# First chunk's scores by pairs of heads on the two halves of the rows, gates added by a selection product

## The chip, the cores and the metric

The kernel runs on one core of a Trainium2 chip. The metric is the device time of one execution in microseconds. PE is TensorE, DVE is VectorE, ACT is ScalarE, POOL is GpSimd, and SP is the engine whose queue issues most DMAs.

## The reference

Attention with forget gates over 2 batches of 8 heads, 576 tokens and 64 dimensions, then a mixture of 4 experts, then a gated layer. All inputs and outputs are float32.

```python
scores = (1 / sqrt(D)) * q @ k.T                       # B, H, S, S = 2, 8, 576, 576; D = 64
cum = cumsum(log(clip(f, 1e-4, 1)), axis=-1)
scores = where(causal, -1e9, scores + cum[..., :, None] - cum[..., None, :])
attn = exp(scores - max(scores)); attn = attn / (sum(attn) + 1e-9)
x = (attn @ v), heads side by side                     # 1152 tokens x 512
p = domain_probs / (sum(domain_probs) + 1e-9)
x = sum over 4 experts e of p[:, e] * (relu(x @ w1[e]) @ w2[e])
h = x @ w_in
out = (h * sigmoid(1.702 * h)) @ w_out
```

The query's own `cum` is the same for a whole row and drops out of the softmax, so the kernel adds only the key's.

## The kernel before

The work is cut into four chunks of tokens: the first 256 and the last 320 tokens of each batch (`CH`, line 20). Attention of a chunk is emitted in units, and the expert layers of a chunk follow when its eight heads are done. Large products are done in three products of rounded parts (`hi` and `lo`, in the type fp32r), the first chunk's scores in plain float32. A scheduling layer orders the instructions of each engine by its own estimate of their durations, so an edit in one place can move instructions in others. Instructions marked with `keep_in_program_order` stay in the order in which they are written.

The gates are prepared on 16 partitions, one per batch and head (lines 638 to 665): clip on DVE, logarithm on ACT, running sum on DVE (`cum`, in the tile `fr`), each in a first part of 256 and a second of 320 columns. After that the scaled sums go to DRAM (`cumd`), from where later chunks read them back to all partitions as `cb` and `cbs`.

The first chunk (`plain(c)`) works as follows. `load_plain` loads q and k of four heads each with 64 partitions as `qd` and `kd`, and v as `vd`. Partition 64 of `qd` holds a constant, and `load_plain_rest` writes the gate sums of four heads into partition 64 of `kd` by a DMA from ACT's queue, so that one product over 65 rows yields the score with its gate. A unit of the first chunk is one head with its two tiles of 128 queries (128 and 256 keys wide):

- `emit_scores` (line 394): the products on PE into one of two PSUM tiles `s`; `emit_max` (line 420): on DVE, mask and scale into `e`, with the row's maximum `mx`;
- `emit_exp` (line 434): on ACT, with the sum into `sm`; `emit_norm` (lines 440 to 443): reciprocal on DVE, and the product with it on POOL (this is called the normalization below);
- `emit_tr` (line 461): transposes on PE, taken to `ph` by ACT or DVE; `emit_pv` (line 491): the second products into `x`; `emit_x2` splits `x` into the halves `xh` and `xl`, and `emit_first` (line 581) multiplies them with the first expert's weights.

In the same stretch POOL rounds the next chunk's q and k (`khi`, `klo`, lines 50 and 333), adds a triangle to `cb` and `cbs` (lines 346 to 355) and sums the expert probabilities (`dps`, lines 259 to 264). Weights come in pairs of blocks as `wst` (line 142) and are split into `whi` (ACT or POOL) and `wlo` (DVE, line 163).

Of the kernel before, what the change touches and what calls it, by code (L numbers as in the profile page):

```python
# [7 lines left out]
F32 = mybir.dt.float32  # L8
# [3 lines left out]
ALU = mybir.AluOpType  # L12
PSUM = bass.MemoryType.PSUM

B, H, S, D = 2, 8, 576, 64
NT = B * S
DM = 512
SA = 256
# [4 lines left out]
WN = 384  # L23
WIDE = [NCH, NCH + 1, NCH + 2]
QW = 640
# [7 lines left out]
def attn_moe_mlp(ctx: ExitStack, tc: tile.TileContext, qk0, qk1, qk2, v0, vp, fg, dp, wa_moe, wb_moe, wa_mlp, wb_mlp, outT):  # L33
# [6 lines left out]
    nc = tc.nc  # L40
# [19 lines left out]
    h_p = pool("h", 2)  # L60
# [228 lines left out]
    def plain(c):  # L289


        return c == 0

    def load_plain(h0):
        G, wk = 4, SA
        qd, kd = ((h_p.tile([128, 4 * WN], F32, tag=t, name=n) if h0 else
                   kq_p.tile([128, S + QW], F32, tag="kq", name=n))[:, :G * wk].rearrange("p (g s) -> p g s", g=G)
                  for n, t in (("qd", "hh"), ("kd", "hl")))
        vd = v_p.tile([128, 2 * G * D], F32, tag="vd0", name="vd", bufs=2).rearrange("p (t g d) -> p t g d", t=2, g=G)
        for i, t in enumerate((kd, qd)):  # L300
            nc.sync.dma_start(out=t[0:64], in_=qk0[h0 // G, i].rearrange("d (g s) -> d g s", g=G))
        nc.sync.dma_start(out=vd, in_=v0[h0 // G].rearrange("p (t g d) -> p t g d", t=2, g=G))

        nc.gpsimd.memset(qd[64:65], 1.0 / NEG)
        groups[h0] = (qd, kd, vd)

    def load_plain_rest(h0):
        G, wk = 4, SA
        qd, kd, vd = groups[h0]
        nc.scalar.dma_start(out=kd[64:65], in_=cum[h0:h0 + G, :wk])  # L310
        for g in range(G):
            heads[0, h0 + g] = dict(vd=vd[:, :, g, :], qd=qd[:65, g], kd=kd[:65, g])

    def load_heads(p, h0):

# [40 lines left out]

    def units_of(c, h0):

        if plain(c):
            return [(c, ((h,), (0, 128))) for h in (h0, h0 + 1)]  # L360
        _, s0, n = CH[c]
        return [(c, ((h0, h0 + 1), (q0,))) for q0 in range(s0, s0 + n, 128)]

    sc, raw_s = {}, {}
    NEG = -1.0 / D ** 0.5

    def emit_scores(c, u):


        hs, tiles = u  # L370
        out = []
        for q0 in tiles:
            w = min(q0 + 128, S)
            if plain(c):
                st = heads[c, hs[0]]
                mm = [(0, w, [(st["qd"][:, q0:q0 + 128], st["kd"][:, :w])])]
            else:
                p = pass_of[c]
                hi, lo = (pairs[p, hs[0]][k] for k in ("hi", "lo"))
                if q0 < 512:  # L380
                    o = S + 128 + q0 - p[2]
                    zs = [(0, w, slice(64 * g, 64 * g + 64)) for g in range(2)]
                else:
                    o = S
                    zs = [(a, z, slice(0, 128)) for a, z in ((0, 288), (288, S))]
                mm = [(a, z, [(l[r, o:o + 128], k[r, a:z]) for l, k in ((hi, hi), (lo, hi), (hi, lo))]) for a, z, r in zs]
            pts = []
            for a, z, _ in mm:
                pts.append(ps_s.tile([128, 512], F32, tag="s", name="s"))
                out.append((q0, w, a, z, pts[-1]))  # L390
            n = len(mm[0][2])
            for i in range(n):
                for pt, (a, z, lr) in zip(pts, mm):
                    nc.tensor.matmul(pt[:, :z - a], lhsT=lr[i][0], rhs=lr[i][1], start=i == 0, stop=i == n - 1)  # L394
        raw_s[c, u] = out

    def emit_max(c, u):
# [77 lines left out]
    def emit_pv(c, h):  # L475

        if h % 2 == 0:
            return
        b, s0, n = CH[c]
        nk = (s0 + n + 127) // 128  # L480
        pt = xf[c, h // 2] = ps_t.tile([128, 512], F32, tag="t", name="x")
        for i in range(nk):
            o = max(0, 128 * i - s0)
            for g in range(2):
                ph = ph_of[c, h - 1 + g]
                if plain(c):
                    lhsT = heads[c, h - 1 + g]["vd"][:, i, :]
                else:
                    lhsT = pairs[pass_of[c], h - 1]["vd"][:, i, g, :]
                rhs = ph[:, i, o:n] if i < 4 else ph[:, 3, 0:64]  # L490
                nc.tensor.matmul(pt[64 * g:64 * g + 64, o:n], lhsT=lhsT, rhs=rhs, start=i == 0, stop=i == nk - 1)  # L491
# [152 lines left out]

    nc.scalar.activation(out=cum[:, :1], in_=ones[:, :1], func=AF.Ln)
    load_plain(0)
    load_plain(4)
    nc.gpsimd.memset(mask, 0.0)
    nc.gpsimd.affine_select(out=mask[:, 128:], in_=mask[:, 128:], pattern=[[-1, 128]],
                            compare_op=ALU.is_ge, fill=-1e10, base=0, channel_multiplier=1)  # L650
# [5 lines left out]
    for a, z in ((0, SA), (SA, S)):  # L656
        nc.vector.tensor_scalar(out=fr[:, a:z], in0=fr[:, a:z], scalar1=1e-4, scalar2=1.0, op0=ALU.max, op1=ALU.min)
        nc.scalar.activation(out=fr[:, a:z], in_=fr[:, a:z], func=AF.Ln)
        nc.vector.tensor_tensor_scan(out=cum[:, a:z], data0=ones[:, a:z], data1=fr[:, a:z],
                                     initial=cum[:, a - 1:a] if a else 0.0, op0=ALU.mult, op1=ALU.add)  # L660
        if a == 0:
            load_plain_rest(0)
            load_plain_rest(4)
    nc.vector.tensor_scalar(out=fr, in0=cum, scalar1=1.0 / NEG, scalar2=None, op0=ALU.mult)
    nc.scalar.dma_start(out=cumd, in_=fr)
    load_heads(passes[1], 0)
# [130 lines left out]
```

## Time and profile before

| | us |
|---|---|
| median of 3 runs | 737.4 |
| lowest of them | 736.33 |
| the profiled execution | 737.77 |
| its span, first to last instruction | 736.1 |
| PE busy | 715.6 (97%) |
| PE weight loads busy | 674.9 (92%) |
| DVE busy | 460.2 (63%) |
| POOL busy | 277.6 (38%) |
| ACT busy | 268.4 (36%) |
| HBM, mean over the span | 90 GB/s |

The busy times are sums over a span of unlike stages. What the first chunk is bound by can't be read from them; it takes the order of events in the first 40 us. A matmul's end is modelled, so the starts of PE's rows say more than their ends. A float32 product shows as two records, a product of the fp32r type as one. A row of the timeline merges instructions that follow one another; the name and shape in it are those of the first.

### The profile page before, as it was taken

Reading aid. Unit: us, or ns where it says so; the run is one execution under the profiler, and the core shown is the slowest. Engines: PE = TensorE matmul, PEld = TensorE weight load, DVE = VectorE, ACT = ScalarE, POOL = GpSimd, SP = SyncE. Lnnn points to the kernel's source line nnn. Section 1 sums busy time; section 2 is a strip of 40 time slices with the busy share of each in tenths; the row PEclk is TensorE's granted clock in tenths of the full one; section 3 lists DMA queues with packets and bytes.
Section 4 is the critical chain, followed back from the end, with each engine's and each line's share of the span. In section 5 each row is a group of like instructions: output and inputs, shape, how many; then the busy total and the mean of one; then the engine's idle time right before and its main releaser. Section 6 shows DMA issues by size and latency. Waiting matters only on the chain.

```text
span 736.1 us, 11924 instructions
## 1 busy us (share of the span) xinstructions
PE 715.6 (97%) x4488; PEld 674.9 (92%) x4488; DVE 460.2 (63%) x1023; ACT 268.4 (36%) x629; POOL 277.6 (38%) x345
## 2 busy tenths in 40 slices
PE   4999999999999999999999999999999999999998
PEld 3576788888899999999998999999999999999997
DVE  4785666575758999999999633445972124424422
ACT  4564554566542233222211221223354433323420
POOL 4886974653432022233232433232462222222220
PEclk9999999999999999999999999999999999999999
DMA  8776534332216464464443301000100000000012
GB/s 290 222 233 208 159 123 132 90 103 86 73 51 216 144 194 149 148 183 117 130 144 115 86 24 35 1 1 1 58 0 1 1 1 1 1 0 1 1 44 86
DMA packets 29496, 67.23 MB, mean 91 GB/s; under 512 B 3032, under 2 KB 4576, under 8 KB 29440
## 3 DMA queue, kind: packets, MB, share of 16 engines
q1 hardware_dynamic: 29392, 66.44, 28.9%
q8 instruction: 35, 0.57, 0.3%
q14 instruction: 21, 0.17, 0.1%
q10 hardware_dynamic: 48, 0.05, 0.0%
HBM read 64.05 MB, written 2.41 MB: 90 GB/s over the span
## 4 chain that ended last, share of the span: by engine, by line
PE 75%; DVE 13%; DMA 5%; issue 3%; POOL 3%; ACT 0%; ACTq 0%; DVEq 0%; POOLq 0%
PE m L604 32%; PE m L560 31%; PE s L394 5%; PE t L461 3%; PE x L491 3%; DVE wlo L163 3%; DMA mst<-in_wa_mlp_dram 2%; DMA mst<-in_wb_mlp_dram 2%; DVE cvd L226 1%; DVE wf L220 1%; DVE cvt L214 1%; DVE tmp L618 1%; DVE cvt L212 1%; DVE hl L587 1%; DVE wf L228 1%
## 5 line engine op out<-in xcount | busy, mean ns | idle before, releaser
L620 POOL TENSOR_TENSOR acc<-acc,tmp 128x384 f32<-128x384 f32 (+3 forms) x112 | 111.2, 1004 | 248.9 <-DVE tmp L618 238.0
L604 PE MATMUL m<-hh,wlo 128*128 128x384 f32 (+2 forms) x640 | 128.0, 320 | 1.4 <-DVE wlo L163 1.3
L604 PE MATMUL m<-hh,whi 128*128 128x384 f32 (+2 forms) x640 | 129.1, 321 | 0.0
L604 PE MATMUL m<-hl,whi 128*128 128x384 f32 (+2 forms) x640 | 127.7, 320 | 0.0
L560 PE MATMUL m<-xh,whi 128*128 128x384 f32 (+2 forms) x624 | 126.1, 322 | 0.4 <-DVE hl L587 0.2
L560 PE MATMUL m<-xl,whi 128*128 128x384 f32 (+2 forms) x624 | 126.2, 321 | 0.0
L560 PE MATMUL m<-xh,wlo 128*128 128x384 f32 (+2 forms) x624 | 126.2, 321 | 0.0
L53 ACT ACTIVATE whi<-wst 128x512 fp32r<-128x512 f32 x103 | 64.9, 631 | 119.8 <-PE m L560 58.0
L163 DVE TENSOR_TENSOR wlo<-wst,whi 128x512 fp32r<-128x512 f32 x112 | 93.3, 836 | 24.3 <-ACT whi L53 13.7
L604 PEld LDWEIGHTS m<-hh,wlo 128*128 128x128 f32 x640 | 105.6, 188 | 3.2 <-DVE wlo L163 2.4
L604 PEld LDWEIGHTS m<-hh,whi 128*128 128x128 f32 x640 | 105.8, 188 | 1.7 <-issue 0.7
L560 PEld LDWEIGHTS m<-xh,whi 128*128 128x128 f32 x624 | 103.1, 188 | 3.7 <-issue 1.7
L604 PEld LDWEIGHTS m<-hl,whi 128*128 128x128 f32 x640 | 105.9, 188 | 0.8 <-issue 0.5
L560 PEld LDWEIGHTS m<-xl,whi 128*128 128x128 f32 x624 | 103.8, 188 | 0.9 <-issue 0.7
L560 PEld LDWEIGHTS m<-xh,wlo 128*128 128x128 f32 x624 | 103.7, 188 | 1.1 <-issue 1.0
L595 POOL TENSOR_TENSOR hl<-tmp,hh 128x384 fp32r<-128x384 f32 x48 | 49.1, 1025 | 133.3 <-ACT hh L53 133.3
L586 ACT ACTIVATE hh<-m 128x384 fp32r<-128x384 f32 (+2 forms) x112 | 48.9, 436 | 117.5 <-PE m L560 117.5
L587 DVE SCALAR_TENSOR_TENSOR hl<-m,hh 128x384 fp32r<-128x384 f32 (+2 forms) x112 | 54.9, 493 | 34.9 <-ACT hh L586 34.9
L618 DVE TENSOR_TENSOR tmp<-m,dpb 128x384 f32<-128x384 f32 (+2 forms) x80 | 40.9, 512 | 38.4 <-PE m L604 32.0
L593 DVE TENSOR_TENSOR tmp<-m,sg 128x384 f32<-128x384 f32 x48 | 26.6, 554 | 54.2 <-ACT sg L592 54.2
L443 POOL TENSOR_SCALAR e<-e,sm 128x128 f32<-128x128 f32 (+4 forms) x72 | 47.4, 668 | 29.4 <-DVE sm L441 15.7
L434 ACT ACTIVATE e<-e,mx 128x128 f32<-128x128 f32 (+4 forms) x72 | 41.9, 583 | 35.9 <-DVE mx L420 34.9
(80 smaller groups left out, 742.6 us busy)
## 6 DMA issues: line engine op xcount, KB each, us to landing
wst<-in_wa_moe_dram SPq DMA_DIRECT2D x28, 512.0 KB, 3.5
wst<-in_wb_moe_dram SPq DMA_DIRECT2D x28, 512.0 KB, 3.8
mst<-in_wa_mlp_dram SPq DMA_DIRECT2D x16, 512.0 KB, 3.5
mst<-in_wb_mlp_dram SPq DMA_DIRECT2D x16, 512.0 KB, 3.6
cb<-cumd SPq DMA_DIRECT2D x16, 256.0 KB, 4.1
vd<-in_vp_dram SPq DMA_DIRECT2D x8, 320.0 KB, 13.1
kq<-in_qk_dram SPq DMA_DIRECT2D x4, 608.0 KB, 7.2
cbs<-cumd SPq DMA_DIRECT2D x8, 288.0 KB
```

Source lines behind the costliest of these rows:

```text
L53: nc.scalar.activation(out=out, in_=in_, func=AF.Copy)
L163: sub = nc.vector.tensor_sub(lf, raw, f(hf))
L394: nc.tensor.matmul(pt[:, :z - a], lhsT=lr[i][0], rhs=lr[i][1], start=i == 0, stop=i == n - 1)
L434: nc.scalar.activation(out=e[:, off:off + w], in_=e[:, off:off + w], func=AF.Exp, scale=-1.0, bias=mx, accum_out=sm[:, 0, k:k + 1])
L443: nc.gpsimd.tensor_scalar(out=e[:, off:off + w], in0=e[:, off:off + w], scalar1=sm[:, 0, i:i + 1], scalar2=1.0, op0=ALU.mult, op1=ALU.mult)
L560: nc.tensor.matmul(p[:, :n], lhsT=w[:, k, :], rhs=x[c][:, k, :], start=(j == 0 and k == 0), stop=(j == 2 and k == 3))
L586: nc.scalar.activation(out=hh[:, g, :n], in_=p[:, :n], func=AF.Relu)
L587: nc.vector.scalar_tensor_tensor(out=hl[:, g, :n], in0=p[:, :n], scalar=0.0, in1=f(hh[:, g, :n]), op0=ALU.max, op1=ALU.subtract)
L595: nc.gpsimd.tensor_sub(hl[:, g, :n], t[:, :n], f(hh[:, g, :n]))
L604: nc.tensor.matmul(p[:, :n], lhsT=w[:, k, :], rhs=x[:, k, :n], start=(j == 0 and k == 0), stop=(j == 2 and k == 3))
L618: nc.vector.tensor_mul(t[:, :n], p[:, :n], d)
L620: nc.gpsimd.tensor_add(a, a, t[:, z])
```

## The change

The gate row and the constant row go. q and k of a pair of heads now lie on the two halves of the partitions (head 0 on 0 to 63, head 1 on 64 to 127), and two pairs come with one DMA. The first chunk's gate sums are copied to partitions 0 to 15 (by ACT) and 64 to 79 (by DVE) of a zeroed tile `cum2`. A tile `sel` holds, for each pair, a row that picks the head's line of `cum2` on its half. A unit of the first chunk is now two heads with one tile of queries, as in the other chunks, and makes four float32 products over 64 rows: `sel` with `cum2` for the first head, for the second, then q with k for the first and for the second. The last three of them are kept in that order.

```diff
-    def load_plain(h0):
-        G, wk = 4, SA
...
-        for i, t in enumerate((kd, qd)):
-            nc.sync.dma_start(out=t[0:64], in_=qk0[h0 // G, i].rearrange("d (g s) -> d g s", g=G))
-        nc.sync.dma_start(out=vd, in_=v0[h0 // G].rearrange("p (t g d) -> p t g d", t=2, g=G))
-
-        nc.gpsimd.memset(qd[64:65], 1.0 / NEG)
-        groups[h0] = (qd, kd, vd)
-
-    def load_plain_rest(h0):
...
-        nc.scalar.dma_start(out=kd[64:65], in_=cum[h0:h0 + G, :wk])
...
+    def load_plain(k):
+
+        t = kq_p.tile([128, S + QW], F32, tag="kq", name="kq0")[:, :4 * SA].rearrange("p (g s) -> p g s", g=2)
+        vd = v_p.tile([128, 8 * D], F32, tag="vd0", name="vd", bufs=2).rearrange("p (t g d) -> p t g d", t=2, g=4)
+        nc.sync.dma_start(out=t, in_=qk0[2 * k:2 * k + 2].rearrange("g p s -> p g s"))
+        nc.sync.dma_start(out=vd, in_=v0[k].rearrange("p (t g d) -> p t g d", t=2, g=4))
...
-        if plain(c):
-            return [(c, ((h,), (0, 128))) for h in (h0, h0 + 1)]
...
-                st = heads[c, hs[0]]
-                mm = [(0, w, [(st["qd"][:, q0:q0 + 128], st["kd"][:, :w])])]
+
+                kq = groups[hs[0]][0]
+                mm = [(0, w, [(sel[r, h // 2, :], cum2[r, :w]), (kq[r, SA + q0:SA + q0 + 128], kq[r, :w])])
+                      for h, r in zip(hs, (slice(0, 64), slice(64, 128)))]
...
-                    nc.tensor.matmul(pt[:, :z - a], lhsT=lr[i][0], rhs=lr[i][1], start=i == 0, stop=i == n - 1)
+                    m = nc.tensor.matmul(pt[:, :z - a], lhsT=lr[i][0], rhs=lr[i][1], start=i == 0, stop=i == n - 1)
+                    if plain(c) and (i or pt is not pts[0]):
+                        tc.keep_in_program_order(m)
...
+    cum2 = h_p.tile([128, 4 * WN], F32, tag="hh", name="cum2")[:, :SA]
+    sel = h_p.tile([128, 4 * WN], F32, tag="hl", name="sel")[:, :4 * 128].rearrange("p (h q) -> p h q", h=4)
+    nc.gpsimd.memset(cum2, 0.0)
+    nc.gpsimd.memset(sel, 1.0 / NEG)
+    for g in range(2):
+        z = slice(64 * g, 64 * g + 64)
+
+        nc.gpsimd.affine_select(out=sel[z], in_=sel[z], pattern=[[-2, 4], [0, 128]], compare_op=ALU.is_equal,
+                                fill=0.0, base=-g, channel_multiplier=1)
...
-            load_plain_rest(0)
-            load_plain_rest(4)
+            nc.scalar.copy(out=cum2[:16], in_=cum[:, :SA])
+            nc.vector.tensor_copy(cum2[64:80], cum[:, :SA])
```

The order of the instructions changes with it. PE at the program's start, before; `s` are score tiles, `t` transposed ones, and a number tells buffers apart:

```order
L394 MATMUL s_175<-kd_131,qd_130 128x128 [waits DMAHW2_49,DMAHW5_49,DMAHW1_49,Pool_49]
L394 MATMUL s_177<-kd_131,qd_130 128x256
L394 MATMUL s_191<-kd_131,qd_130 128x128 [waits DVE_49]
L394 MATMUL s_193<-kd_131,qd_130 128x256 [waits DVE_49]
L394 MATMUL s_215<-kd_131,qd_130 128x128 [waits DVE_49]
L461 MATMUL t_202<-identr_124,e_179 128x128 [waits Pool_49]
```

PE at the same place now:

```order
L383 MATMUL s_175<-cum2_138,sel_139 128x128 [waits Activation_49,Pool_49]
L383 MATMUL s_176<-cum2_138,sel_139 128x128 [waits DVE_49,Pool_49]
L383 MATMUL s_175<-kq0_130 128x128 [waits DMAHW1_49]
L383 MATMUL s_176<-kq0_130 128x128
L383 MATMUL s_193<-cum2_138,sel_139 128x256 [waits DVE_49]
L383 MATMUL s_194<-cum2_138,sel_139 128x256 [waits DVE_49]
L383 MATMUL s_193<-kq0_130 128x256
L383 MATMUL s_194<-kq0_130 128x256
L452 MATMUL t_207<-identr_124,e_181 128x128 [waits Pool_49]
```

The first product waited for three DMAs and POOL; now it waits for ACT and POOL, the second for DVE and POOL, and only the third for a DMA.

POOL from its first normalization on, before (`khi` and `klo` are the next chunk's rounded keys and queries):

```order
L443 TENSOR_SCALAR e_179<-e_179,sm_180 128x128 [waits DVE_49,Activation_49]
L443 TENSOR_SCALAR e_179<-e_179,sm_180 128x256 [waits Activation_49]
L50 TENSOR_SCALAR khi_280<-kq_160 128x576 [waits DMAHW2_49]
L50 TENSOR_SCALAR khi_280<-kq_160 128x384
L333 TENSOR_TENSOR klo_281<-kq_160,khi_280 128x576 [waits Pool_49]
L443 TENSOR_SCALAR e_195<-e_195,sm_196 128x128 [waits DVE_49,Activation_49]
L443 TENSOR_SCALAR e_195<-e_195,sm_196 128x256 [waits Activation_49]
L333 TENSOR_TENSOR klo_281<-kq_160,khi_280 128x384 [waits Pool_49]
```

POOL from its first normalization on, now:

```order
L434 TENSOR_SCALAR e_181<-e_181,sm_182 128x128 [waits DVE_49,Activation_49]
L434 TENSOR_SCALAR e_181<-e_181,sm_182 128x128 [waits Activation_49]
L50 TENSOR_SCALAR khi_290<-kq_160 128x576 [waits DMAHW5_49]
L50 TENSOR_SCALAR khi_290<-kq_160 128x384
L322 TENSOR_TENSOR klo_291<-kq_160,khi_290 128x576 [waits Pool_49]
L322 TENSOR_TENSOR klo_291<-kq_160,khi_290 128x384 [waits Pool_49]
L434 TENSOR_SCALAR e_199<-e_199,sm_200 128x256 [waits DVE_49,Activation_49]
L434 TENSOR_SCALAR e_199<-e_199,sm_200 128x256 [waits Activation_49]
L259 TENSOR_TENSOR dps_339<-dpraw_169 128x9 [waits DMAHW2_49]
L261 TENSOR_TENSOR dps_339<-dps_339,dpraw_169 128x9 [waits Pool_49] x2
L434 TENSOR_SCALAR e_225<-e_225,sm_226 128x128 [waits DVE_49,Activation_49]
```

The second unit's normalization stood behind three of the four pieces of rounding and is now behind all four.

DVE around the first weight splits (`wlo`), before; line 420 is a maximum, with a second instruction that reads it out:

```order
L420 ISA e_274,mx_276<-s_270,ones_126 128x128 [waits Pool_49]
L420 ISA mx_276 128x1
L420 ISA e_274,mx_278<-s_272,ones_126 128x256
L420 ISA mx_278 128x1
L163 TENSOR_TENSOR wlo_650<-wst_171,whi_649 128x512 [waits DMAHW7_49,Activation_49]
L163 TENSOR_TENSOR wlo_653<-wst_171,whi_652 128x512 [waits Activation_49]
L440 TENSOR_SCALAR sm_275<-sm_275 128x2 [waits Activation_49]
L468 COPY ph_256<-t_260 128x2x128 [waits PE_49]
L441 RECIPROCAL sm_275<-sm_275 128x2 [waits DVE_49]
L263 RECIPROCAL dps_327<-dps_327 128x9 [waits Pool_49]
L420 ISA e_316,mx_318<-s_312,ones_126 128x128 [waits PE_49]
```

DVE around the first weight splits, now (`e_251` is the fourth unit's, `ph_205` and `ph_206` are the second unit's transposed tiles):

```order
L459 COPY ph_205<-t_231 128x2x128 [waits PE_49]
L263 RECIPROCAL dps_339<-dps_339 128x9 [waits Pool_49]
L163 TENSOR_TENSOR wlo_666<-wst_171,whi_665 128x512 [waits DMAHW3_49,Activation_49]
L163 TENSOR_TENSOR wlo_669<-wst_171,whi_668 128x512 [waits Activation_49]
L411 ISA e_251,mx_253<-s_245,ones_126 128x256 [waits PE_49]
L411 ISA mx_253 128x1
L163 TENSOR_TENSOR wlo_672<-wst_173,whi_671 128x512 [waits DMAHW4_49,Activation_49]
L163 TENSOR_TENSOR wlo_675<-wst_173,whi_674 128x512 [waits Pool_49]
L411 ISA e_251,mx_255<-s_246,ones_126 128x256 [waits PE_49]
L411 ISA mx_255 128x1
L459 COPY ph_206<-t_235 128x2x128 [waits PE_49]
```

The splits came behind the fifth head's maxima; now two stand ahead of each of the fourth unit's two maxima.

## Rows read from the trace of the kernel before

**Rows 1.** Busy time by stretch: bounds, length, busy us (instructions), granted clock, DMA, GB/s.

```profile
20.00:30.00 10.00, 9.39 (x45) 5.38 (x44) 7.84 (x32) 5.91 (x23) 9.60 (x21) 1.00 0.70 220
...
200.00:400.00 200.00, 199.71 (x1358) 196.08 (x1358) 182.93 (x356) 56.27 (x116) 52.52 (x52) 1.00 0.46 142
```

**Rows 2.** Timeline of PE from 9 us: start, length, instruction, count, idle before.

```profile
10.13 3.79 PE L394 MATMUL s<-kd,qd 65*128 65x128 f32 x10 [10.13 <-DMA cumd<-fr]
```

**Rows 3.** Timeline of ACT and its DMA queue (ACTq), 0 to 14 us.

```profile
4.72 1.81 ACTq L310 DMA_DIRECT2D kd<-fr  x2
...
7.05 1.28 ACT L434 ACT_TABLE_LOAD   x1 [2.58 <-DVE fr L664]
11.26 0.40 ACT L434 ACTIVATE e<-e,mx 128x128 f32<-128x128 f32 x1 [2.93 <-DVE mx L420]
...
12.25 0.51 ACT L434 ACTIVATE e<-e,mx 128x256 f32<-128x256 f32 x1 [0.49 <-DVE mx L420]
```

**Rows 4.** Timeline of DVE, 0 to 30 us.

```profile
3.89 1.78 DVE L659 TENSOR_TENSOR_SCAN fr<-ones,fr 16x256 f32<-16x256 f32 x2
5.71 0.45 DVE L664 TENSOR_SCALAR fr<-fr 16x576 f32<-16x576 f32 x1
10.93 0.29 DVE L420 CUSTOM_DVE_ANT_0 e<-s,ones 128x128 f32<-128x128 f32 x1 [4.78 <-PE s L394]
...
11.79 0.42 DVE L420 CUSTOM_DVE_ANT_0 e<-s,ones 128x256 f32<-128x256 f32 x1 [0.56 <-PE s L394]
...
15.70 0.42 DVE L468 COPY ph<-t 128x256 f32<-128x256 f32 x1
...
20.09 1.38 DVE L163 TENSOR_TENSOR wlo<-wst,whi 128x512 fp32r<-128x512 f32 x2
```

**Rows 5.** Timeline of POOL, 0 to 40 us.

```profile
2.42 0.29 POOL L649 TENSOR_SCALAR_AFFINE_SELECT ones<-ones 128x128 f32<-128x128 f32 x1
...
13.43 0.82 POOL L443 TENSOR_SCALAR e<-e,sm 128x128 f32<-128x128 f32 x2 [8.64 <-DVE sm L441]
14.22 1.15 POOL L50 TENSOR_SCALAR khi<-kq 128x576 fp32r<-128x576 f32 x2
15.33 1.41 POOL L333 TENSOR_TENSOR klo<-kq,khi 128x576 fp32r<-128x576 f32 x1
...
17.51 1.00 POOL L333 TENSOR_TENSOR klo<-kq,khi 128x384 fp32r<-128x384 f32 x1
...
20.25 1.28 POOL L261 TENSOR_TENSOR dps<-dps,dpraw 128x9 f32<-128x9 f32 x2
...
37.48 0.82 POOL L443 TENSOR_SCALAR e<-e,sm 128x128 f32<-128x128 f32 x2
```

**Rows 6.** DMA issues, whole span and 0 to 45 us: count, size, us to landing.

```profile
wst<-in_wa_moe_dram SPq DMA_DIRECT2D x28, 512.0 KB, 3.5
...
kd<-in_qk_dram SPq DMA_DIRECT2D x2, 256.0 KB, 3.6
```

**Rows 7.** PE's groups by shape, 10 to 21.9 us, then 21.9 to 30 us: busy, mean ns.

```profile
L394 PE MATMUL s<-kd,qd 65*128 65x256 f32 x10 | 5.7, 676 | 0.1
L394 PE MATMUL s<-kd,qd 65*128 65x128 f32 x10 | 3.3, 434 | 10.1 <-DMA cumd<-fr 10.1
...
L394 PE MATMUL s<-kd,qd 65*128 65x256 f32 x6 | 1.9, 397 | 0.0
L394 PE MATMUL s<-kd,qd 65*128 65x128 f32 x6 | 1.4, 308 | 0.0
```

**Rows 8.** Timeline of PE, next chunk's scores: 42 us, then 59 us.

```profile
42.16 0.44 PE L394 MATMUL s<-khi 64*128 64x384 f32 x1
...
59.18 0.44 PE L394 MATMUL s<-khi 64*128 64x384 f32 x2
59.46 0.34 PE L394 MATMUL s<-khi,klo 64*128 64x384 f32 x2
59.63 0.34 PE L394 MATMUL s<-klo,khi 64*128 64x384 f32 x2
```

More of the change, by code (lines that the diff above doesn't have):

```diff
@@ L292, in plain @@
         return c == 0
-    def load_plain(h0):
-        G, wk = 4, SA
[L296 to L299, printed above, removed]
-        for i, t in enumerate((kd, qd)):
-            nc.sync.dma_start(out=t[0:64], in_=qk0[h0 // G, i].rearrange("d (g s) -> d g s", g=G))
-        nc.sync.dma_start(out=vd, in_=v0[h0 // G].rearrange("p (t g d) -> p t g d", t=2, g=G))
-        nc.gpsimd.memset(qd[64:65], 1.0 / NEG)
-        groups[h0] = (qd, kd, vd)
-    def load_plain_rest(h0):
-        G, wk = 4, SA
-        qd, kd, vd = groups[h0]
-        nc.scalar.dma_start(out=kd[64:65], in_=cum[h0:h0 + G, :wk])
-        for g in range(G):
-            heads[0, h0 + g] = dict(vd=vd[:, :, g, :], qd=qd[:65, g], kd=kd[:65, g])
+    def load_plain(k):
[4 more added lines that the diff above has]
+        for g in range(2):
+            groups[4 * k + 2 * g] = (t[:, g], vd[:, :, 2 * g:2 * g + 2, :])
     def load_heads(p, h0):
@@ L486, in emit_pv @@
                 if plain(c):
-                    lhsT = heads[c, h - 1 + g]["vd"][:, i, :]
+                    lhsT = groups[h - 1][1][:, i, g, :]
                 else:
@@ L646, in attn_moe_mlp @@
     load_plain(0)
-    load_plain(4)
+    load_plain(1)
+    cum2 = h_p.tile([128, 4 * WN], F32, tag="hh", name="cum2")[:, :SA]
+    sel = h_p.tile([128, 4 * WN], F32, tag="hl", name="sel")[:, :4 * 128].rearrange("p (h q) -> p h q", h=4)
+    nc.gpsimd.memset(cum2, 0.0)
+    nc.gpsimd.memset(sel, 1.0 / NEG)
+    for g in range(2):
+        z = slice(64 * g, 64 * g + 64)
+        nc.gpsimd.affine_select(out=sel[z], in_=sel[z], pattern=[[-2, 4], [0, 128]], compare_op=ALU.is_equal,
+                                fill=0.0, base=-g, channel_multiplier=1)
     nc.gpsimd.memset(mask, 0.0)
@@ L759, in first @@
     def first(k, q):
-        a = np.stack([k[0, :, :SA], q[0, :, :SA]]).reshape(2, 2, 4, SA, D)
-        return a.transpose(1, 0, 4, 2, 3).reshape(2, 2, D, 4 * SA)
+        return np.concatenate([a[0, :, :SA].transpose(0, 2, 1).reshape(4, 2 * D, SA) for a in (k, q)], axis=-1)
     def pairs(k, q, s0):
```

## Prediction

> **What bounds the kernel now.** I read the table of stretches first. From 200 us to 400 us PE is busy for 199.71 of 200 us [rows 1]: there the end is the sum of PE's work, and any gain has to be made earlier. The order of the two programs agrees: their last 3,016 products on PE, nearly all of what comes behind 200 us, are the same in the same order. So the change can move the end only by moving the moment at which PE reaches that common stretch.
>
> I then read the start, engine by engine. PE's first product begins at 10.13 us, after a wait that fills the whole time before it [rows 2]. The row names the DMA of `cumd` as releaser, but the product waits for the loads of `kd` and `qd` and for the gate row written into `kd` by ACT's queue. DVE has the first half of the scan by about 4.7 us (the scan row starts at 3.89 us and holds both halves, 1.78 us together), ACT's queue issues the two gate DMAs between 4.72 us and 6.53 us, and the loads of q and k, issued from 1.26 us on, take 3.6 us [rows 3, 4, 6]. So the gate DMA comes last: 5.4 us pass between the scan's first half and the first product.
>
> After that, two views matter. POOL waits 8.64 us for its first normalization at 13.43 us and is then nearly never free: 9.60 of the 10 us from 20 to 30 us [rows 1, 5]. Its last normalization of the first chunk ends at 38.30 us (37.48 us + 0.82 us) [rows 5]. I take that moment as the mark by which a lead of the new kernel is measured, because PE's transposes, the second products and the first expert's products follow it. And PE is slow until about 21.9 us: a 256-column record of the scores lasts 676 ns before and 397 ns after, a 128-column one 434 ns and 308 ns [rows 7]. [...]
>
> **The change part by part.**
>
> *The gate DMAs go; a copy on ACT and one on DVE replace them.* An activation of 128 columns took 0.40 us, a copy of 256 columns on DVE 0.42 us [rows 3, 4]. The two run side by side behind the scan's first half, so `cum2` is ready at about 4.7 + 0.05 + 0.42 = 5.2 us. The other inputs: q and k of the first four heads now come in one DMA of 512 KB, issued at the same 1.26 us; the nearest rows are 3.5 us to landing for the weight loads of that size and 3.6 us for the load of `kd` [rows 6], so 4.8 to 4.9 us, at worst 6 us since it is twice as large as the latter. The selection tile needs two selections of 512 columns on POOL, whose first selection of 128 columns began at 2.42 us and took 0.29 us [rows 5]; a wider one costs between 0.29 and 4 x 0.29 = 1.16 us, so the tile is ready between 3.3 and 5.0 us and hides. I take 5.9 us for PE's first product: 4.2 us earlier.
>
> *What gives back the first part.* ACT's second table load stood behind the issue of `cumd` and began at 7.05 us for 1.28 us [rows 3]. The issue waits for DVE's scaled gates, which ended at 6.16 us and now come 0.42 us later because the copy stands ahead of the second half of the scan [rows 4]. The two gate issues that went before it cost 1.81 us of ACT's queue and are gone, but they were not last. So the table is still in place only at about 8.3 us, and the first exponential starts there instead of at 11.26 us. From the first exponential to POOL's first normalization it was 13.43 - 11.26 = 2.17 us, 0.49 us of which ACT waited for a second maximum [rows 3, 5]; in the new unit both maxima (0.29 us each) are there by then. First normalization: 8.3 + 2.17 - 0.49 = 10.0 us, a lead of 3.4 us.
>
> *The products.* A pair of heads had two products per tile, one behind the other, over 65 rows. It now has four, in the order selection of the first head, selection of the second, q of the first, q of the second, the two heads on different halves of the rows. Where the old kernel alternates such halves, its trace shows both at once: six 384-column products begin as three pairs at 59.18, 59.46 and 59.63 us, and the first pair of them lasts the same 0.44 us that a single one takes at 42.16 us [rows 8]. So I cost the 16 added products at nothing. If the halves did not overlap, they would be as dear as the 16 there are: 5.7 + 3.3 + 1.9 + 1.4 = 12.3 us of PE [rows 7].
>
> Going from 128-row to 64-row products is not free: the first of those steps lasts 59.46 - 59.18 = 0.28 us, the second 59.63 - 59.46 = 0.17 us [rows 8]. Transposes and second products use all 128 rows, so the eight units make some nine changes in and nine out: 18 x 0.11 = 2.0 us at the upper clock, which were not there before. I take none of it, since a unit's second pair waits for DVE's maxima anyway, and keep 2.0 us for the range. [...]
>
> *What the new order gives back later.* A lead of 3.4 us on POOL would reach the mark whole if nobody waited. The order shows a knot at the fourth unit (second tile of heads 2 and 3). POOL now does all four pieces of the next chunk's key rounding before the second unit's normalization: 1.15 + 1.41 + 1.00 = 3.56 us [rows 5]. With the first unit's normalization (0.8 us, the row for 128 and 256 columns is 0.82 us) that makes 10.0 + 0.8 + 3.56 = 14.4 us; then the second unit's (0.9 us by the same row, for 512 columns), the probability sums (1.28 us) and the third unit's (0.7 us, for 256): 17.3 us. The transposes that wait for the second unit stand on PE between the two selection products of the fourth unit. On DVE the probabilities' reciprocal, which needs POOL at 17.3 us, stands ahead of two weight splits (1.38 us), the fourth unit's first maximum (0.42 us), two more splits (1.38 us) and the second maximum (0.42 us) [rows 4, 5]: 17.3 + 3.6 us, and an estimated 0.3 us for the reciprocal and the steps between, make 21.2 us. In the old trace DVE has five heads' maxima and two splits behind it at 20.09 + 1.38 = 21.5 us [rows 4]; now it has four heads and four splits at 21.2 us. Two splits more (1.38 us) and one head less (0.29 + 0.42 us) make 0.7 us, and 0.3 us in time: a lead of about 1.0 us.
>
> So between 1.0 us (DVE's order sets the mark) and 3.4 us (POOL alone does). POOL's fourth normalization needs DVE's fourth pair of maxima, so the lower end is nearer: I take 1.5 us. DMA bytes stay as they were; the stretch behind the mark is shuffled by the scheduler, with the same work in it, at nothing.
>
> *The sum.* The profiled execution took 737.77 us (span 736.1 us); 737.77 - 1.5 = 736.3 us. The median of the runs is 0.4 us lower than that execution, inside what I can resolve.
>
> **The rivals.**
>
> *The lead passes whole* (chance 0.25): the knot dissolves because POOL waits less elsewhere. For it: POOL is the fullest engine from 20 to 30 us. Against it: DVE's splits stand ahead of POOL's next input. 737.77 - 3.4 = 734.4 us.
>
> [...]
>
> *The halves don't overlap* (0.05), the change not doing what it says: half of the 12.3 us is hidden at best, so 737.77 - 1.5 + 6 to 12 = 742 to 748 us. Rows 8 speak against it.
>
> **How the numbers follow.** My forecast, 736.3 us with a range of its own from 734.8 to 738.2 us, has 0.50; the whole lead 0.25, the slower knot 0.17, no overlap 0.05, the rest 0.03. The range from 731.0 us (whole lead and an earlier clock) to 740.5 us (the knot) leaves out the lack of overlap and the rest. Two per cent, about what a measurement of this kernel can tell from no change, is 14.8 us; no case but the last reaches it. Faster 0.02, same 0.95, slower 0.03.
>
> **What would show it.** Right: the first score product near 5.9 us, ACT's second table load still near 7 us, POOL's first normalization near 10 us, score products of the two heads starting together, and the first chunk's last normalization between 35 and 37.5 us. Wrong: a first product near 10 us (loads were last, not the gates), products one behind the other, a fourth unit's maximum well before 19 us or after 23 us, or the common stretch reached with a lead or lag other than at the mark.

## The result, and the profile after

The changed kernel takes 744.88 us (median; 742.53 to 746.58), the kernel before 737.22 us beside it: a ratio of 1.0091, 95% interval 1.0063 to 1.0118. (One of the old kernel's four executions took 1168.98 us; without it their median is 737.04 us.) The change is slower by 7.7 us: less than the 2% (14.8 us) that I took as the least a measurement can tell, but clear of the noise by its interval, and outside my range. The profiled execution is the slowest of the four, 746.58 us (span 744.9 us), so its waits may be somewhat longer than those of a median execution.

The table of stretches of the changed kernel, with the columns of [rows 1]:

```profile
0.00:13.00 13.00, 5.58 (x26) 3.91 (x26) 6.71 (x22) 6.47 (x16) 7.49 (x19) 1.00 0.84 307
...
20.00:30.00 10.00, 9.40 (x51) 6.03 (x51) 5.27 (x27) 4.60 (x19) 8.02 (x17) 1.00 0.45 134
30.00:40.00 10.00, 4.43 (x15) 2.72 (x16) 3.28 (x11) 1.09 (x4) 4.07 (x9) 0.69 0.69 198
40.00:60.00 20.00, 20.00 (x126) 15.21 (x127) 11.81 (x46) 11.38 (x31) 11.48 (x20) 0.90 0.46 162
...
200.00:400.00 200.00, 199.07 (x1356) 194.81 (x1356) 178.52 (x355) 58.15 (x122) 55.55 (x54) 1.00 0.46 142
```

The same stretch of 30 to 40 us in the kernel before:

```profile
30.00:40.00 10.00, 9.08 (x48) 5.79 (x47) 7.13 (x23) 3.75 (x11) 7.60 (x14) 1.00 0.73 220
```

One row stands out. From 30 to 40 us PE is busy for 4.43 us (9.08 us before), POOL for 4.07 us, and the granted clock is 0.69 of full: it reads 1.00 in every stretch up to 33 us and 0.50 in each microsecond from 34 to 44 us (0.95 in the one ahead, 0.93 in the one behind). Below, the lower level is this 0.50, or a stretch in which records last as long as there: a 256-column second product (`x<-ph,vd`) takes 653 ns (mean) from 33.9 to 44.1 us, 671 ns from 10 to 22 us, where the clock reads 1.00, and 404 ns from 46 to 60 us. From 20 to 30 us PE is as busy as it was (9.40 us against 9.39 us), and the common stretch behind 200 us is nearly as full (199.07 us against 199.71 us) [rows 1]. The timeline of PE shows the start and the stall:

```profile
4.93 0.90 PE L383 MATMUL s<-cum,sel 64*128 64x128 f32 x4 [4.93 <-ACT cum L663]
...
20.19 0.58 PE L383 MATMUL s<-cum,sel 64*128 64x128 f32 x1 [0.47 <-DVE mx L411]
20.19 0.58 PE L383 MATMUL s<-kq 64*128 64x128 f32 x1
...
23.21 1.23 PE L383 MATMUL s<-cum,sel 64*128 64x256 f32 x4
24.23 1.06 PE L383 MATMUL s<-kq 64*128 64x256 f32 x4
...
28.45 0.70 PE L383 MATMUL s<-cum,sel 64*128 64x256 f32 x4
28.99 0.60 PE L383 MATMUL s<-kq 64*128 64x256 f32 x4
35.23 1.14 PE L452 MATMUL t<-identr,e 128*128 128x128 f32 x4 [5.65 <-POOL e L434]
36.27 0.58 PE L572 MATMUL m<-xh,whi 128*128 128x256 f32 x1
...
57.39 0.73 PE L551 MATMUL m<-xh,whi 128*128 128x256 f32 x4
```

The first product starts at 4.93 us, 5.2 us before the old one [rows 2], released by the copy on ACT. Products of the two heads start together (20.19 us). Then PE stands 5.65 us at 29.6 us for a normalization by POOL. POOL's own timeline says why:

```profile
9.41 0.72 POOL L434 TENSOR_SCALAR e<-e,sm 128x128 f32<-128x128 f32 x2 [4.75 <-DVE sm L432]
...
21.37 0.94 POOL L434 TENSOR_SCALAR e<-e,sm 128x256 f32<-128x256 f32 x2 [1.21 <-DVE mx L411]
...
28.95 0.45 POOL L338 TENSOR_TENSOR cb<-cb,tri 128x128 f32<-128x128 f32 x1
33.90 0.70 POOL L344 TENSOR_TENSOR cbs<-cbs,tri 64x64 f32<-64x64 f32 x2 [4.50 <-DMA cbs<-cumd]
34.70 0.93 POOL L434 TENSOR_SCALAR e<-e,sm 128x256 f32<-128x256 f32 x2
...
36.19 1.15 POOL L434 TENSOR_SCALAR e<-e,sm 128x128 f32<-128x128 f32 x2
...
39.79 0.93 POOL L434 TENSOR_SCALAR e<-e,sm 128x256 f32<-128x256 f32 x2 [1.86 <-DVE sm L432]
```

The first normalization comes 4.0 us earlier than in [rows 5]. By the fourth unit's normalization this lead is gone: four heads are then normalized at 22.31 us (21.37 + 0.94 us). In the kernel before, the same four heads were done at 20.28 us:

```profile
19.46 0.82 POOL L443 TENSOR_SCALAR e<-e,sm 128x128 f32<-128x128 f32 x2
```

POOL had other work in between (the next `khi` at 18.15 us, which the old kernel has at 29.16 us). Then POOL stands 4.50 us at the triangle add on `cbs` for that tile's load, and the first chunk's last three normalizations come behind it in its row: DVE had the reciprocals of the first two by 27.35 and 29.22 us, and they begin at 34.70 and 36.19 us. The last ends at 40.72 us, where the old kernel's ended at 38.30 us [rows 5].

The kernel before has the same late load, in its POOL and PE timelines:

```profile
35.29 0.71 POOL L355 TENSOR_TENSOR cbs<-cbs,tri 64x64 f32<-64x64 f32 x2 [2.25 <-DMA cbs<-cumd]
```

```profile
30.58 0.38 PE L581 MATMUL m<-xh,whi 128*128 128x256 f32 x1
...
49.27 0.50 PE L560 MATMUL m<-xh,whi 128*128 128x256 f32 x2
```

There only the last head's normalizations stand behind the add, and PE has the first expert's products to do. So the lag is 36.27 - 30.58 = 5.7 us at the first expert's first product (L572, before L581) and 57.39 - 49.27 = 8.1 us at the first product of the common code (L551, before L560). At the end it is 8.8 us (spans of 744.9 us and 736.1 us).

### The profile page after: what moved, and what is told of

Read it like the earlier page. It is cut to its first block, busy times and chain, and to the rows that moved or that the text cites. A ratio compares the mean times of both kernels' runs of the same rounds, so it can differ in the third digit from the quotient of the medians.

```text
span 744.9 us, 11979 instructions
## 1 busy us (share of the span) xinstructions
PE 720.9 (97%) x4520; PEld 679.1 (91%) x4520; DVE 457.2 (61%) x1024; ACT 269.0 (36%) x630; POOL 277.3 (37%) x347
## 4 chain that ended last, share of the span: by engine, by line
PE 61%; DVE 15%; DMA 12%; POOL 6%; issue 5%; ACT 0%; ACTq 0%; SPq 0%; DVEq 0%; POOLq 0%
PE m L595 28%; PE m L551 26%; DMA mst<-in_wb_mlp_dram 5%; DMA mst<-in_wa_mlp_dram 4%; PE s L383 3%; DVE wlo L163 3%; DVE cvd L226 2%; PE x L482 2%; DVE cvt L212 2%; PE t L452 2%; POOL klo L322 2%; POOL e L434 2%; DVE cvt L214 1%; DVE cvt L223 1%; DMA cbs<-cumd 1%
## 5 line engine op out<-in xcount | busy, mean ns | idle before, releaser
L551 PE MATMUL m<-xh,whi 128*128 128x384 f32 (+2 forms) x624 | 127.2, 323 | 0.9 <-DVE hl L578 0.8
L551 PE MATMUL m<-xh,wlo 128*128 128x384 f32 (+2 forms) x624 | 126.0, 321 | 0.0
L551 PE MATMUL m<-xl,whi 128*128 128x384 f32 (+2 forms) x624 | 124.9, 320 | 0.0
L551 PEld LDWEIGHTS m<-xh,whi 128*128 128x128 f32 x624 | 103.1, 188 | 4.6 <-issue 2.3
L551 PEld LDWEIGHTS m<-xh,wlo 128*128 128x128 f32 x624 | 103.8, 188 | 0.6 <-issue 0.4
L551 PEld LDWEIGHTS m<-xl,whi 128*128 128x128 f32 x624 | 103.6, 188 | 0.4 <-issue 0.4
L434 POOL TENSOR_SCALAR e<-e,sm 128x128 f32<-128x128 f32 (+4 forms) x72 | 45.0, 636 | 33.2 <-DVE sm L432 25.9
```

What stands on the lines that cost most here:

```text
L434: nc.gpsimd.tensor_scalar(out=e[:, off:off + w], in0=e[:, off:off + w], scalar1=sm[:, 0, i:i + 1], scalar2=1.0, op0=ALU.mult, op1=ALU.mult)
L551: nc.tensor.matmul(p[:, :n], lhsT=w[:, k, :], rhs=x[c][:, k, :], start=(j == 0 and k == 0), stop=(j == 2 and k == 3))
```

## Experiments

Theory A: POOL's row, with a `cbs` add that waits for a slow load ahead of the normalizations, makes the loss. Rival B: the new products make it (changes between halves, records at the lower level at the start). Times are medians; each run is compared with the kernel before, timed on the same chip at 735.9 to 738.0 us.

**Each `cbs` load as two DMAs**

```diff
-nc.sync.dma_start(out=st["cbs"], in_=cumd[r:r + 2, :].unsqueeze(1).to_broadcast([2, 64, S]))
+for g in range(2):
+    nc.sync.dma_start(out=st["cbs"][64 * g:64 * g + 64], in_=cumd[r + g:r + g + 1, :].to_broadcast([64, S]))
```

> The changed kernel, and each load of cbs (the gates of a head pair, one head to each half of 64 rows) written as two DMAs of 64 rows instead of one whose source is two rows with 64 copies each. Nothing else is edited. Theory A (the late cbs load): in the changed kernel GpSimd stands 4.50 us at 29.40 us behind the triangle add on cbs, with the normalizations of the first chunk's last units queued behind it, TensorE waits 5.65 us for them and falls to the lower clock. Two DMAs land sooner, so these waits should nearly go (together under 1.5 us), the first product of the first expert should start at 30 to 32 us instead of 36.27, and the time should be 735 to 739 us. Rival B (the new products themselves: the half-row pairs with their changes of tile, or the lower clock at the start that is left 5 us later): the wait of GpSimd may go, and the time stays at 742 to 746.

Measured: 736.23 us, ratio 0.9967 (0.9948 to 0.9985). With the order of POOL's row unchanged, the waits have nearly gone (POOL, then PE):

```profile
28.95 0.45 POOL L338 TENSOR_TENSOR cb<-cb,tri 128x128 f32<-128x128 f32 x1
29.36 0.70 POOL L345 TENSOR_TENSOR cbs<-cbs,tri 64x64 f32<-64x64 f32 x2
30.15 0.93 POOL L435 TENSOR_SCALAR e<-e,sm 128x256 f32<-128x256 f32 x2
```

```profile
30.69 0.97 PE L453 MATMUL t<-identr,e 128*128 128x128 f32 x4 [1.50 <-POOL e L435]
31.73 0.58 PE L573 MATMUL m<-xh,whi 128*128 128x256 f32 x1
```

The load itself is seen in one stretch of the table (last two columns: share of the 16 DMA engines, GB/s), first of the changed kernel, then of this one:

```profile
25.00:26.00 1.00, 1.00 (x6) 0.71 (x4) 0.68 (x3) 0.15 (x1) 1.00 (x3) 1.00 0.13 51
```

```profile
25.00:26.00 1.00, 1.00 (x8) 0.78 (x10) 0.98 (x5) 0.46 (x2) 1.00 (x3) 1.00 1.02 268
```

As one DMA it shows a share of 0.13, so some seven eighths of the DMA time are unused; as two, and with the loads behind it under way as well, the share is 1.02. Two of 16 engines, busy throughout, would make a share of 0.125; which engines moved its pieces, and why, is not shown.

B falls as the main cause: its products are all still there. Behind what is left of PE's wait, 1.50 us, the clock still falls (granted 0.66 from 30 to 40 us, 0.50 from 32 to 36 us).

This kernel is not ahead at the start:

```profile
52.26 0.74 PE L552 MATMUL m<-xh,whi 128*128 128x256 f32 x4
```

PE reaches the first expert 1.1 us and the common code 3.0 us later than in the kernel before, and yet the span is 2.2 us shorter (733.9 us against 736.1 us). From 60 to 200 us PE is idle for 0.04 us here, for 3.2 us in the kernel before and 4.2 us in the changed one. So the split does more than take the first wait away: of the 11.0 us of span that it wins from the changed kernel (744.9 - 733.9), some 4 us lie behind the first chunk.

**The same edit in the kernel before**

> The kernel before with the same edit alone: each cbs load as two DMAs of 64 rows. In the kernel before GpSimd waits 2.25 us for cbs at 35.29 us, with one normalization behind it and expert products for TensorE to go on with. Theory A: little to win here, 734 to 738 us, so that the edit repairs the changed kernel and does not merely make any kernel faster by 1%. Rival C (the slow load costs every kernel the same, by the bandwidth it holds): 727 to 731 us, as much won here as in the changed kernel.

Measured: 738.3 us, ratio 1.0007 (0.9982 to 1.0033). Rival C falls: the edit repairs the changed kernel and does not make every kernel faster. That the slow load costs the old kernel nothing is not shown, because POOL's row came out another way here: PE has a new wait of 1.00 us for a normalization, up to 37.66 us, with a granted clock of 0.86 from 30 to 40 us, which may hide a small gain.

**Slow load kept, POOL's row re-ordered** (in `prep_cum`, `emit_max` and `emit_norm`)

```diff
     st["cbs"] = cbs_p.tile([128, S], F32, tag="cbs", name="cbs")
...
-    for g in range(2):
-        z = slice(64 * g, 64 * g + 64)
-        nc.gpsimd.tensor_add(st["cbs"][z, 512:], st["cbs"][z, 512:], tri[z, z])
...
     nc.gpsimd.memset(e[:, S:640], 0.0)
+    for g in range(2):
+        y = slice(64 * g, 64 * g + 64)
+        d = nc.gpsimd.tensor_add(st["cbs"][y, 512:], st["cbs"][y, 512:], tri[y, y])
+        if (c, u[0][0]) in ((1, 0), (1, 2)):
+            tc.keep_in_program_order(d)
...
-    nc.gpsimd.tensor_scalar(out=e[:, off:off + w], in0=e[:, off:off + w], scalar1=sm[:, 0, i:i + 1],
+    d = nc.gpsimd.tensor_scalar(out=e[:, off:off + w], in0=e[:, off:off + w], scalar1=sm[:, 0, i:i + 1],
...
+    if plain(c):
+        tc.keep_in_program_order(d)
```

> The changed kernel with its slow cbs load left as it is; the triangle add on cbs is moved in GpSimd's row to just ahead of the first use of cbs, so that all normalizations of the first chunk stand ahead of it (the four normalizations that stood behind the two first cbs adds move up). Theory A: the row's order, not the load, is what hurts; TensorE's wait of 5.65 us at 29.6 shrinks to under 2 us, the first expert's first product starts at 30 to 33 us, time 736 to 740 us, as with the split load or up to 2 us longer where the cbs add then delays the later chunk. Rival B: 742 to 746 us. Rival D (the load's bandwidth hurts other loads, not GpSimd's row): also 742 to 746 us here, though the split load helps.

Measured: 740.92 us, ratio 1.004 (1.002 to 1.006): 2.9 us above the kernel before (738.04 us beside it) instead of 7.7 us. PE no longer waits in the first chunk, and starts the first expert at 29.95 us. But it waits later, where POOL's row is held up at a `cb` add:

```profile
29.95 0.37 PE L576 MATMUL m<-xh,whi 128*128 128x256 f32 x1
...
47.52 1.12 PE L456 MATMUL t<-identr,e 128*128 128x128 f32 x4 [3.18 <-POOL e L436]
48.28 0.56 PE L576 MATMUL m<-xh,whi 128*128 128x256 f32 x1
```

```profile
44.81 0.45 POOL L335 TENSOR_TENSOR cb<-cb,tri 128x128 f32<-128x128 f32 x1 [5.51 <-DVE mx L413]
```

The row names DVE, but the add also needs its own load, in the pair issued from 37.53 us on; the eight `cb` loads of this run that were issued from 10 to 60 us land 10.5 us after their issue (median), and which of the two came last is not shown. So theory A holds for the first stall, and its "736 to 740 us" was too low: the lateness moved on. (The profiled execution, 744.06 us, is the slowest of this run.)

**Both edits**

> The changed kernel with both edits: each cbs load as two DMAs, and the triangle add on cbs placed behind the first chunk's normalizations. With the split load alone TensorE still waited 1.50 us at 29.2 us and ran at the lower clock until about 40 us; with the moved add alone it did not wait in the first chunk, but 3.18 us at 44.3 us for a row of GpSimd held up by late loads. Theory A: both waits go, no fall of the clock between 27 and 60 us, first expert's first product at 29.5 to 30.5 us, time 731 to 735 us. Rival B2 (the clock falls all the same, from what TensorE does there, not from the wait): 736 to 738 us, with 128x256 products at 0.41 us in the records somewhere between 30 and 45 us.

Measured: 734.29 us, ratio 0.9953 (0.9933 to 0.9974). No wait of PE between 20 and 60 us is over 0.33 us, the granted clock is 1.00 in every stretch up to 600 us, and this version beats both kernels.

```profile
28.40 0.93 POOL L437 TENSOR_SCALAR e<-e,sm 128x256 f32<-128x256 f32 x2
```

```profile
29.98 0.39 PE L577 MATMUL m<-xh,whi 128*128 128x256 f32 x1
...
47.73 0.74 PE L556 MATMUL m<-xh,whi 128*128 128x256 f32 x4
```

PE reaches the first expert 0.6 us and the common code 1.5 us before the old kernel.

**The late order put into the kernel before**

```diff
 for k in new:
     prep_parts(*k)
-    prep_cum(*k)
+    if k != nxt[1]:
+        prep_cum(*k)
+    if k == nxt[0]:
+        pairs[nxt[1]] = {}
+        prep_cum(*nxt[1])
```

> The kernel before, with no change to its score products: only the gates of the second head pair (two cb loads and the cbs load, with their triangle adds) are written three units earlier, beside those of the first pair, so that in GpSimd's row the second cbs add stands ahead of the first chunk's last three normalizations (of four heads' units: six instructions), as it does in the changed kernel. Theory A: this row alone makes the loss; GpSimd waits 3 to 6 us near 29 to 34 us, TensorE waits for a normalization and the time goes to 740 to 745 us. Rival B (the loss is of the new products): 736 to 739 us.

Measured: 741.19 us, ratio 1.0064 (1.0044 to 1.0084), with not one new product (the loads of these gates move up in SP's queue as well). The rows of the changed kernel come back (POOL, then PE):

```profile
33.47 0.70 POOL L355 TENSOR_TENSOR cbs<-cbs,tri 64x64 f32<-64x64 f32 x2 [4.62 <-DMA cbs<-cumd]
```

```profile
34.69 1.14 PE L461 MATMUL t<-identr,e 128*128 128x128 f32 x3 [4.81 <-POOL e L443]
```

So the order without any new product makes 4.4 us over the kernel before (736.82 us beside it), more than half of the loss of 7.7 us, and the split load, which takes the wait away, removes all of it.

**The pin**

```diff
-if plain(c) and (i or pt is not pts[0]):
-    tc.keep_in_program_order(m)
```

> The changed kernel without the pinned order of a tile's four products: TensorE then has the two products of one head, then the two of the other, so that the halves hardly run side by side. GpSimd's row is still held up by the cbs add. Theory A: the stall stays, TensorE still waits 4 to 6 us at about 30 us; the score products take longer by some 8 x 0.5 us in all, mostly hidden in that wait; 743 to 748 us. Rival B (the changes of tile between halves, one at each pinned product, cost the time): with fewer of them the time falls to 737 to 741 us.

Measured: 744.78 us, ratio 1.009 (1.0057 to 1.0122), as with the pin. The time is theory A's, its wait is not: PE is busy from 13 to 36 us with no gap over 0.16 us and begins the first expert at 36.81 us, so the slower products (2.0 us for one head's 256-column tile, 23.29 to 25.29 us) fill the time in which PE would have waited. With POOL's stall in place the products' order costs nothing in the end. Without the stall it is another matter:

> The kernel with both edits (cbs as two DMAs, its triangle add behind the first chunk's normalizations), and without the pin on a tile's four products, so that the halves hardly overlap. Without the pin, but with GpSimd's stall, TensorE was busy from 13 to 36 us without a gap, so the products had become as late as the stall. Theory A (the overlap of the halves is worth 3 to 4 us once the stall is gone): first product of the first expert at 33 to 35 us instead of about 30, time 737 to 740 us. Rival (the overlap is worth nothing, the first chunk waits for VectorE and GpSimd anyway): 733 to 736 us.

Measured: 750.21 us, ratio 1.0164 (1.0124 to 1.0204), 16 us above the same kernel with the pin, far more than I had expected. PE's timeline:

```profile
23.92 1.22 PE L381 MATMUL s<-cum,sel 64*128 64x256 f32 x2
24.93 1.06 PE L381 MATMUL s<-kq 64*128 64x256 f32 x2
...
26.54 1.22 PE L381 MATMUL s<-cum,sel 64*128 64x256 f32 x2
27.55 1.06 PE L381 MATMUL s<-kq 64*128 64x256 f32 x2
...
39.41 0.58 PE L575 MATMUL m<-xh,whi 128*128 128x256 f32 x1
...
46.61 0.41 PE L575 MATMUL m<-xl,whi 128*128 128x256 f32 x1
...
51.64 0.28 PE L575 MATMUL m<-xh,whi 128*128 128x256 f32 x1
```

The two products of one head's 256-column tile take 2.0 us (23.92 to 25.92 us), and those of the other head another 2.0 us behind them (26.54 to 28.54 us). With the pin all four take 2.0 us together, as in the changed kernel (23.21 to 25.22 us). The first expert starts 9.4 us later than with the pin, and a 256-column product of it lasts 0.41 us until 46.6 us and 0.28 us from 51.6 us. In the changed kernel `m<-xl,whi` takes 415 ns (mean) from 33.9 to 44.1 us, at the granted 0.50: PE's records last as at the lower level about twice as long as with the pin, where they shorten at about 25.5 us.

**Both edits in the kernel before**

> The kernel before with both edits (cbs as two DMAs, its triangle add behind the first chunk's normalizations), with its old score products. Theory A (the change's earlier start is worth 1 to 4 us once nothing holds up GpSimd's row): 736 to 739 us, so 2 us or more above the changed kernel with the same edits, 734.3. Rival (the gain is that of the two edits, not of the change): 733 to 735 us.

Measured: 739.94 us, ratio 1.0038 (1.001 to 1.0066), 5.6 us above the changed kernel with the same edits. Part of that is a new wait of the old products: in its profile PE stands 1.71 us at 50.4 us for a maximum by DVE, and the granted clock is 0.91 from 40 to 60 us. The two were timed on different chips (the kernel before took 736.57 and 736.82 us beside them). Against the kernel before as it was, the change with both edits wins 2.5 us.

**The clock: the wait filled with unused products** (`FILL` is 20, then 12; in `emit_tr`)

```diff
+if plain(c) and hs[0] == 4 and q0 == 128 and k == 0:
+    for _ in range(FILL):
+        tc.keep_in_program_order(
+            nc.tensor.matmul(pt[:, 256:512], lhsT=ident, rhs=cum2, start=True, stop=True))
```

> The changed kernel with 20 products added that compute nothing which is used (128x256 float32, into an unused part of a transposition's tile), placed in TensorE's row at the point where it waits 5.65 us. The wait itself stays, as does GpSimd's stall; only the idleness of TensorE goes. Theory A with the clock (about 3 us of the 8.6 us lost are the lower clock from 33.9 to 44.1 us): the clock does not fall there, first product of the first expert still at 36 to 37 us, but the time falls to 740 to 742 us. Rival (the wait alone makes the loss): 744 to 746 us.

> The changed kernel as it is, timed beside the next one on the same chip. Both theories: 743 to 746 us, TensorE's wait of 5 to 6 us near 29.6 us, lower clock after it.

> The changed kernel with the 20 unused products in TensorE's wait, again, now beside the changed kernel. Its first six executions (741.4 to 746.4, median 743.5) overlap those of the changed kernel. If the lower clock is a part of the loss, the median lies 2 to 4 us under that of the changed kernel; if the wait alone is, within 1 us of it.

> The changed kernel with 12 unused products in TensorE's wait instead of 20. The 20 lasted 8.90 us (29.31 to 38.1 us, 0.445 us each), so they reached some 2.5 us beyond the end of the wait and made TensorE late themselves; 12 last 5.3 us and end just inside it. GpSimd's stall stays, and so does the moment at which TensorE goes on (35 to 36 us); the clock is kept up. If the lower clock (34 to 44 us) is a part of the loss, the time is 739.5 to 742 us, against 743.9 to 744.9 for the changed kernel; if the stall alone makes the loss, 743.5 to 746 us.

Measured: the changed kernel again 743.89 us (1.0087, 1.0054 to 1.0121); with 20 unused products 743.48 and 745.34 us; with 12, 749.75 us (1.0183, 1.0157 to 1.021). By their medians the first three are one time, and the last missed both expectations. The traces say why. Stretch of 40 to 60 us with 20 products, then with 12:

```profile
40.00:60.00 20.00, 19.17 (x138) 14.61 (x138) 12.67 (x45) 13.51 (x38) 12.76 (x21) 1.00 0.50 162
```

```profile
40.00:60.00 20.00, 18.88 (x106) 14.05 (x107) 9.74 (x38) 9.19 (x25) 10.22 (x18) 0.75 0.38 130
```

PE's row is the same in both but for those eight products. The 20 lasted 8.90 us and made PE late themselves: the first expert began at 38.83 and 39.30 us, not at the expected 36 to 37 us. The 12 ended before POOL was ready, and PE waited three times:

```profile
35.55 0.89 PE L457 MATMUL t<-identr,e 128*128 128x128 f32 x4 [1.14 <-POOL e L435]
37.82 0.78 PE L384 MATMUL s<-khi 64*128 64x384 f32 x2 [1.38 <-DVE mx L412]
41.12 0.80 PE L577 MATMUL m<-xh,whi 128*128 128x256 f32 x2 [1.27 <-POOL whi L51]
```

The mean granted clock of 0.75 over these 20 us is that of some 10 us at 0.50 and 10 us at 1.00, an estimate; with the 20 it read 1.00. The first expert began at 38.88 us instead of 39.30 us and the median is 4.4 to 6.3 us higher, on another chip.

How much of the changed kernel's loss is the lower clock? Its work from 35.23 to 40 us, 4.4 us, ran at a granted clock of 0.50, and so did some 4 us of that from 40 to 60 us (0.50 from 40 to 44 us): 8.4 us in all. Four products of a 256-column tile pair take 2.01 us where records last as at the lower level (23.21 to 25.22 us) and 1.14 us later (28.45 to 29.59 us), a difference of 0.43 of the longer time; 0.43 of 8.4 us is some 3.6 us, an estimate. The executions do not settle it. Of the 13 with 20 products, the eight with a mean granted clock of 0.999 or more took 741.42 to 744.86 us, the four with 0.995 took 745.98 to 746.79 us. But with the late order in the kernel before, the four with 0.999 or more took 738.93 to 744.55 us and the six with 0.990 or 0.991 took 740.49 to 743.30 us: no difference. With 20 products PE goes on 2.6 to 3.0 us later than in the changed kernel (36.27 us) and the median is hardly later, which speaks for a share of the clock. No run took the fall away and left all else, so the share stays open.

## Why the prediction was wrong

*First product.* Predicted 5.9 us, measured 4.93 us: the gates came at 4.9 us as worked out (5.2 us); q and k were there for their product at 5.49 us, where I had taken the load to be last.

*Table load and first normalization.* Table at 6.66 us (about 7 predicted), normalization at 9.41 us (10.0 us). The lead there was 4.0 us against 3.4 us. Right.

*The products at nothing.* Right as made: with the pin the two heads' products run side by side (20.19 us). "The halves don't overlap" had a chance of 0.05 and 742 to 748 us; without the pin and without the stall it took 750.21 us, with records that last as at the lower level until 46.6 us as well. The 18 changes of rows (2.0 us, taken as nothing, from rows at 59 us, where the granted clock reads 1.00) were not measured by themselves, and the step of 0.11 us that I took for their price is not shown to be one. In the trace of the kernel before, three 128-row products behind another 128-row product (from 34.48 us on) start 0.24 us and then 0.13 us apart, the same step with no change of rows.

*The knot.* On DVE it was milder than I feared. The fourth unit's second maximum was done at about 20.1 us (it begins at 19.71 us) against 21.2 us, by the prediction's own measure a lead of 2 us instead of 1.0 us. On POOL the scheduler had already spent it: the fourth unit's normalization ended 2.0 us later than that of the same heads in the kernel before (22.31 against 20.28 us).

*The step that failed* is the one sentence "DMA bytes stay as they were; the stretch behind the mark is shuffled by the scheduler, with the same work in it, at nothing", and with it the term of 1.5 us for the lead at the mark. The shuffle began ahead of the mark. The second `cbs` add moved in POOL's row from ahead of the last unit's normalization to ahead of the last three, and its load takes about 17.4 us from issue to the add in both kernels (issued at 16.56 us, add at 33.90 us; before, 17.92 and 35.29 us). So that add set the mark: 40.72 us instead of 35 to 37.5 us. I had costed the bytes of that load but not its time, though the old trace shows POOL waiting 2.25 us for it at 35.29 us. Moving that add up makes 4.4 us of loss in the old kernel (741.19 us), and the split load, with which the add no longer waits, takes the whole loss from the new one (736.23 us), some 4 us of it behind the first chunk.

*The mark itself* fell short as a measure. It came 2.4 us late (40.72 against 38.30 us), which by the prediction's rule would be a loss of 2.4 us; the end came 8.8 us late. The sum had no term for PE running dry: PE stood 5.65 us for the transposes' input, and some 3.6 us more, by the estimate above, are the lower clock behind that. How the two add up with the later waits is not worked out.

*Luck.* The split load gives 736.23 us and both edits 734.29 us, close to my 736.3 us and to the 734.4 us of "the lead passes whole". Neither bears the prediction out: the first reaches the common code 3.0 us later than the kernel before and gains behind 60 us, the second reaches it 1.5 us earlier, not 3.4 us.

*The clock in the range.* The upper end (740.5 us, the knot, at 0.17) was my estimate for a clock that rises later than in the kernel before, and the lower end has "an earlier clock". No run shows such a rise: the granted clock reads 1.00 in every stretch up to 33 us in both kernels. What the runs show in its place is the length of the records: the 256-column score products at 23.21 us are still slow (the four of a tile pair take 2.01 us there and 1.14 us at 28.45 us), where those of the kernel before last 397 ns, not 676 ns, from 21.9 us on [rows 7]. But the two faster versions, with the split load and with both edits, are late too (their records shorten at about 24.5 and 25.5 us), so it does not make the loss; what it costs was not measured. The fall that came with the loss is another one: behind POOL's stall from 29.4 us on PE stood from 29.6 us, and at 33.9 us the granted clock fell from 1.00 to 0.50.

## What to carry to other kernels

When a change makes an engine's inputs earlier, look at every instruction in its row that waits for a DMA: the DMA need not come earlier (some 17.4 us from issue to the add in both kernels here), and what a scheduler now places behind that instruction can inherit its wait, as a normalization did here whose reciprocal was ready at 27.35 us and which began at 34.70 us. Take the landing time of each such load from the old trace, even where the wait there cost nothing. And before paying for a slow load by re-ordering, see whether it fills the DMA engines at all (a share of 0.13 here). A mark on one engine measures the end only as long as the engine that bounds the kernel does not run dry on the way to it: here it came 2.4 us late and the end 8.8 us.

## What the runs showed of the hardware

The load of `cbs` as one DMA has two source rows with 64 copies each (288 KB). From 21 to 23 us only pieces of such loads move (two are under way), at 51 to 53 GB/s and a DMA share of 0.13. Split, with the loads behind it under way as well, the stretch of 25 to 26 us shows 268 GB/s and a share of 1.02, and the halves land 5.3 us after their issue (median). The small write of `dpT` behind it in SP's queue landed 17.0 us after its issue, and 6.3 us with the split, where it stands behind only the first pair of halves.

The granted clock reads 1.00 in stretches where records last as at the lower level: in the kernel with both edits and no pin it reads 1.00 up to 60 us, while 256-column products last 0.41 us until 46.6 us although PE was busy for 6.95 of the 7 us from 13 to 20 us and without a gap from 20 to 60 us. In the same kernel with the pin, records shorten at about 25.5 us (four transposes take 0.78 us from 25.01 us on; 1.11 us from 25.22 us on in the changed kernel). What makes them shorten is not shown.
